# Conv and gated feed-forward on one core: the order of loads, casts and first convolutions in the opening

## The chip, the cores and the metric

The kernel runs on one NeuronCore of a Trainium2 chip. The metric is the device time in microseconds of one execution; the time before is 726.78 us, the median of five runs (726.22 to 727.24). The engines are TensorE (PE; its weight loads are shown as PEld), VectorE (DVE), ScalarE (ACT), GpSimd (Pool) and SyncE (SP). SP and ACT also issue the DMA transfers here, each from its own queue of instructions (SPq and ACTq in the profile).

## What is computed

A causal convolution of seven taps with softmax weights for each head, and then a feed-forward layer whose activation is h cos h:

```python
w = exp(weight - max) / sum                      # 8 heads x 7 taps, softmax over the taps
x_pad = concat(zeros(B, 6, D), x)                # B 8, S 4096, D 192, head h has 24 channels
a[b, s, h] = sum_k w[h, k] * x_pad[b, s + k, h]
h = a @ w_in                                     # 32768 x 192  @  192 x 2048
g = h * cos(h)
out = g @ w_out                                  # 2048 x 192
```

## The kernel before, in words

The 32768 tokens are 64 tiles of T = 512, two to a unit of 1024, so 32 units (NU). A unit is loaded as x_f (128 partitions, eight blocks of 128 tokens, and a ninth "edge" block with the 16 tokens around each block's start, which supplies the taps that reach back over the block's edge), cast to bf16 as x_bf (`cast_unit`, L182), and convolved on PE against `band`, a matrix with the tap weights on its diagonals (`conv_mm`, L195). The result goes from PSUM to `ct` by ACT (`conv_out`), Pool doubles it (`double_unit`, since the row halves of the array each want a copy), and a DMA transpose issued by SP turns it into `cT` (`turn_unit`), with channels on the partitions. Pool then mends the first six tokens of each block from the edge block.

For each tile there are eight pairs of feature blocks, j = 0 to 7. `mm1` (named h0 to h7 in the order strings) computes a pair into one of three double banks of PSUM, the ring `h_pool`; `gcu` (s0 to s7) takes its cosine on ACT into `cs` and multiplies on DVE into `g`, after which the ring's buffer is free. `mm2_step` (m with a count) multiplies g by w_out into two banks, o_p and o_q, a step at a time, one row half of the array for each of two phases that overlap. `evac` (P and Q) copies a finished bank to SBUF by ACT, and SP stores it.

The order is written by hand: PE_ORDER and ACT_ORDER from the third tile on, PE_FIRST and ACT_FIRST (L398, L400) for the first two. In these strings c1, c2 are the two parts of the convolution of channel half 1 and d1, d2 of channel half 0; ec and ed are their copies out of PSUM by ACT; r is `conv_rest`; p and q mark the ends of phases. A string's item is issued when those before it have been issued, and every engine works through its own instructions in that order. In the first tile (t = 0) the convolutions of unit 1 use the two o banks, so c waits for d's copies, and the first m steps wait for c's.

Where two matmuls on different row halves would add to the same bank, `Turn` (L166) orders them through SP: a no-operation on SP waits for the first matmul, and the second waits for it. That no-operation stands in SP's queue among its DMA issues, in program order.

The opening, which the change touches, is written out before the loop. Transfers: SP issues the first half of unit 0 (four blocks, 384 KB), half 0 of w_in's first half, the rest of unit 0, unit 1 (768 KB), its edges, the second half of w_in in two transfers (each fills 64 partitions, `load_w` L84), w_out in four. ACT issues the conv weights and half 1 of w_in's first half. PE runs matmuls on zeros (`keep_warm`, L112) and one small matmul that spreads the conv weights. Pool builds a mask and an identity; DVE, with one Exp on ACT (L154), computes the softmax, then `prod` and `diag` (L269, L272), and 16 small copies by the three engines place the diagonals into `band` (L277). ACT casts the first half of unit 0, Pool the second. DVE and Pool cast the first half of w_in (L281). Then `conv_first` convolves four blocks (L293) with copies by ACT and DVE (L299), `turn_first` transposes them on PE (L307), and the first tile starts. Pool's order from there: cast of unit 1 (L326), double of unit 0's second half, the second half of w_in (L435, all 1536 columns in one), w_out in two halves (L437).

Of the kernel before, what the change touches and what calls it, by code (L numbers as in the profile page):

```python
# [9 lines left out]
BF16 = mybir.dt.bfloat16  # L10
AF = mybir.ActivationFunctionType
# [5 lines left out]
def kernel(  # L17
# [8 lines left out]
    nc = tc.nc  # L26
    B, S, D = x.shape
    H, K = weight.shape
# [36 lines left out]
    x_tiles = {}  # L65


    def load_edges(u):
        nc.sync.dma_start(out=x_tiles[u][:, UB, :],  # L69
                          in_=xf[u * U - 8 : u * U - 8 + U, :].rearrange("(n t) d -> n t d", t=128)[:, 0:16, :])  # L70

    def load_unit(u, n0=0, n1=UB):
        if n0 == 0:
            x_tiles[u] = xin.tile([128, UB + 1, D], FP32, name="x_f")
        nc.sync.dma_start(out=x_tiles[u][:, n0:n1, :],  # L75
                          in_=xf[u * U + n0 * 128 : u * U + n1 * 128, :].rearrange("(n p) d -> p n d", p=128))


# [1 line left out]
    w_src = moe_w_in.rearrange("(m k) (t f) -> t m k f", k=NC, t=2)  # L80
    HP = NP // 2


    def load_w(q, queues):  # L84
        for t in range(2):
            queues[t].dma_start(out=w_f[64 * t : 64 * t + 64, :, q * HP : (q + 1) * HP, :].rearrange("p k j f -> p k (j f)"),
                              in_=w_src[t, :, :, q * HP * 128 : (q + 1) * HP * 128])

    load_unit(0, 0, NB)
    load_w(0, [nc.sync, nc.scalar])  # L90
    load_unit(0, NB, UB)
    load_unit(1)
    load_edges(1)
    load_w(1, [nc.sync, nc.sync])
    wo_f = consts.tile([128, NP, 2, D], FP32)
    wo_src = moe_w_out.rearrange("(i j p) d -> p j i d", i=2, p=128)

# [14 lines left out]
    def keep_warm(n):  # L112
        for _ in range(n):
            nc.tensor.matmul(out=idle, lhsT=zero[:, 0:128], rhs=zero, start=True, stop=True)  # L114
# [7 lines left out]
                            channel_multiplier=32)  # L122
    scrap = consts.tile([128, 1], FP32)
    nc.scalar.activation(out=scrap, in_=one, func=AF.Exp)  # L124
    keep_warm(3)
    w_all = o_pools[1].tile([128, T], FP32, name="o_ps1")
    w_bc = w_all[:, 0 : HQ * K].rearrange("p (h k) -> p h k", k=K)
    nc.tensor.matmul(out=w_all[:, 0 : HQ * K], lhsT=quarter, rhs=w_row, start=True, stop=True)
    keep_warm(17)


    xb0 = xbf_pool.tile([128, UB + 1, D], BF16, name="x_bf")

    E = 32 + K - 1
    mask = consts.tile([128, E, K], BF16)
    nc.gpsimd.memset(mask[0:32], 0.0)
    nc.gpsimd.affine_select(out=mask[0:32], in_=mask[0:32], compare_op=ALU.not_equal, fill=1.0, base=1 - K,
                            pattern=[[1, E], [1, K]], channel_multiplier=-1)
    for q in range(1, 4):
        nc.gpsimd.tensor_copy(out=mask[32 * q : 32 * q + 32], in_=mask[0:32])  # L140
    nc.gpsimd.memset(xb0[:, 0, :], 0.0)
    ident = consts.tile([128, 128], BF16)
    nc.gpsimd.memset(ident, 0.0)
    nc.gpsimd.affine_select(out=ident, in_=ident, compare_op=ALU.not_equal, fill=1.0, base=0, pattern=[[1, 128]],
                            channel_multiplier=-1)
    wn = consts.tile([128, HQ, K], BF16)
    band = consts.tile([128, H, 256], BF16)
    nc.vector.memset(band, 0.0)

    wmax = consts.tile([128, HQ, 1], FP32)  # L150
    nc.vector.tensor_reduce(out=wmax[:, :, 0], in_=w_bc, axis=mybir.AxisListType.X, op=ALU.max)
    wexp = consts.tile([128, HQ, K], FP32)
    nc.vector.tensor_tensor(out=wexp, in0=w_bc, in1=wmax.to_broadcast([128, HQ, K]), op=ALU.subtract)
    nc.scalar.activation(out=wexp, in_=wexp, func=AF.Exp)  # L154
    wsum = consts.tile([128, HQ, 1], FP32)
    nc.vector.tensor_reduce(out=wsum[:, :, 0], in_=wexp, axis=mybir.AxisListType.X, op=ALU.add)
    winv = consts.tile([128, HQ, 1], FP32)
# [21 lines left out]

    bf = {}  # L180

    def cast_unit(u, n0=0, n1=UB + 1):  # L182
        copy = nc.scalar.copy if u == 0 and n0 == 0 else nc.gpsimd.tensor_copy
        bf[u] = xb0 if u == 0 else xbf_pool.tile([128, UB + 1, D], BF16, name="x_bf")

        o = 1 if u == 0 else 0
        copy(out=bf[u][:, n0 + o : n1 + o, :].rearrange("p n (h k r) -> p (n h) k r", k=NC, r=R),  # L187
             in_=x_tiles[u][:, n0:n1, :].rearrange("p n (h r k) -> p (n h) k r", k=NC, r=R))
        if u and u % UPS == 0:
            nc.gpsimd.memset(bf[u][0:8, UB, :], 0.0)  # L190
        bf.pop(u - 2, None)
# [27 lines left out]
    def o_banks():  # L219
        return [o_pools[b].tile([128, T], FP32, name="o_ps%d" % b) for b in range(2)]  # L220

    def conv_part(u, c, banks):


        ps = banks()
        sides = [slice(0, 64), slice(64, 128)]

        def mm(i, rows, **flags):
            return conv_mm(u, c, ps, i, sides[rows], 0, UB + 1, **{"start": False, "stop": False, **flags})

        mm(0, 0, start=True)
        mm(2, 1, start=True)
        turn = Turn()
        turn.mark(mm(1, 0), mm(3, 1))
        yield
        turn.wait(mm(2, 0), mm(0, 1))
        mm(3, 0, stop=True)
        mm(1, 1, stop=True)
        yield
        if c == 0 and u not in ct_tiles:  # L240
            ct_tiles[u] = ct_pool.tile([128, UB + 1, NC, 2, 64], BF16, name="ct")
        for b in range(2):
            conv_out(u, c, ps, 0, 0, UB + 1, nc.scalar.copy, banks=(b,))
            yield
# [7 lines left out]
    def turn_unit(u, n0=0, n1=UB + 1):  # L252
        ct = ct_tiles.pop(u)
        if u not in cT:
            cT[u] = cT_pool.tile([128, UB + 1, NC, 128], BF16, name="cT")
        nc.sync.dma_start_transpose(out=cT[u][:, n0:n1].rearrange("p n c k -> p (n c) k"),
                                    in_=ct[:, n0:n1].rearrange("p n c t k -> p (n c t k)"))
        cT.pop(u - 2, None)

    def mend_edges(u):  # L260
# [2 lines left out]
                              in_=cT[u][:, UB].rearrange("p c (n t) -> p n c t", t=16)[:, :, :, 8 : 8 + K - 1])  # L263


    cast_unit(0, 0, NB)

    prod = consts.tile([128, HQ, E, K], BF16)
    nc.vector.tensor_tensor(out=prod, in0=mask.rearrange("p (o e) k -> p o e k", o=1).to_broadcast([128, HQ, E, K]),  # L269
                            in1=wn.rearrange("p h (o k) -> p h o k", o=1).to_broadcast([128, HQ, E, K]), op=ALU.mult)  # L270
    diag = consts.tile([128, HQ, E], FP32)
    nc.vector.tensor_reduce(out=diag, in_=prod, axis=mybir.AxisListType.X, op=ALU.add)  # L272
# [2 lines left out]
    for i in range(16):  # L275
        q, rows = divmod(i, 4)
        three[i % 3](out=band[32 * rows : 32 * rows + 32, HQ * q : HQ * (q + 1), 32 * rows : 32 * rows + E],  # L277
                     in_=diag[32 * q : 32 * q + 32])
    nc.scalar.activation(out=scrap, in_=one, func=AF.Sin)
    for k in range(NC):  # L280
        three[2 if k else 0](out=w[:, k, 0:HP], in_=w_f[:, k, 0:HP])  # L281
    cast_unit(0, NB, UB)
    ct_tiles[0] = ct_pool.tile([128, UB + 1, NC, 2, 64], BF16, name="ct")
    cT[0] = cT_pool.tile([128, UB + 1, NC, 128], BF16, name="cT")
# [38 lines left out]
    conv_first()  # L323
    turn_first(0)
    turn_first(1)
    cast_unit(1)  # L326
    load_unit(2)
    load_edges(2)


    g_tiles = {}
# [54 lines left out]
    def store(t, b0=0, b1=2):  # L386
# [8 lines left out]
    PE_ORDER = "h0 m7 c1 m6 c2 m4 h1 m7 q h2 h3 m12 h4 m10 h5 m10 h6 h7 p m8"  # L395
    ACT_ORDER = "s0 ec1 ec2 s1 Q s2 s3 s4 s5 P s6 s7"

    PE_FIRST = ["h0a h0b h1 r d1 h2 d2 h3 h4 h5 h6 c1 h7 c2 p m12",  # L398
                "h0 m8 h1 m12 q h2 h3 h4 m4 d1 m8 d2 h5 m8 h6 c1 m8 c2 h7 m4 p m8"]
    ACT_FIRST = ["s0a s0b s1 s2 ed1 ed2 s3 s4 s5 s6 ec1 ec2 s7", "s0 s1 s2 s3 s4 ed1 ed2 s5 s6 ec1 ec2 P s7"]  # L400

    HALVES = {"": (0, NB), "a": (0, NB // 2), "b": (NB // 2, NB)}
    step = 0
    for t in range(NT + 2):
        u, second = divmod(t, TPU)
        cu, cc = (u + TPU, second) if t >= TPU else (1 + t, 1)
        conv = {"c": conv_part(cu, cc, ring_banks if t else o_banks) if cu < NU else iter(())}
        if t < TPU:
            conv["d"] = conv_part(cu, 0, ring_banks if t else o_banks)
        act, done, h = (ACT_ORDER if t > 1 else ACT_FIRST[t]).split(), set(), {}  # L410

        def flush():
# [14 lines left out]

        for k in (PE_ORDER if t > 1 else PE_FIRST[t]).split():
            if k[0] == "h" and t < NT:
                h[k[1:]] = mm1(t, int(k[1]), *HALVES[k[2:]])  # L430
            elif k[0] in conv:
                next(conv[k[0]], None)
                if (t, k) == (0, "d1"):
                    turn_unit(0, NB, UB)
                    nc.gpsimd.tensor_copy(out=w[:, :, HP:NP], in_=w_f[:, :, HP:NP])  # L435
                    for q in range(2):
                        nc.gpsimd.tensor_copy(out=wo[:, q * HP : (q + 1) * HP], in_=wo_f[:, q * HP : (q + 1) * HP])  # L437
            elif k == "r":
                conv_rest()
                double_unit(0, NB, UB)  # L440
            elif k[0] == "m":
                for q in range(step, step + int(k[1:])):
                    mm2_step(q)
                step += int(k[1:])
            elif k[0] == "p":
                assert step % (2 * STEPS) == 0
            elif k[0] == "q":
                assert step % (2 * STEPS) == STEPS
            done.add(k)
# [61 lines left out]
```

## Time and profile before

| | us |
|---|---|
| median of five runs | 726.78 |
| the profiled execution's own time | 726.69 |
| span of its profile, first to last instruction | 725.0 |
| PE busy, share of the span | 711.7, 98% |
| DVE busy | 611.3, 84% |
| ACT busy | 618.0, 85% |
| Pool busy | 152.0, 21% |
| granted TensorE clock, mean | 0.995 |

How to read it: every line of a timeline has its start and its length in us from the first instruction, then engine, line, operation and the tiles written and read, and in square brackets how long the engine stood idle before and what it waited for. A chain line has start, length and what the time was spent on. A line of busy time by stage has the stage, its length, the busy us (and count) of PE, PEld, DVE, ACT and Pool, the granted share of the TensorE clock, the share of the 16 DMA engines that were busy, and GB/s. Ends of matmuls are modelled, so neighbouring PE lines overlap a little.

### The profile page before, as it was taken

Reading aid. Unit: us, or ns where it says so; the run is one execution under the profiler, and the core shown is the slowest. Engines: PE = TensorE matmul, PEld = TensorE weight load, DVE = VectorE, ACT = ScalarE, POOL = GpSimd, SP = SyncE. Lnnn points to the kernel's source line nnn. Section 1 sums busy time; section 2 is a strip of 40 time slices with the busy share of each in tenths; the row PEclk is TensorE's granted clock in tenths of the full one; section 3 lists DMA queues with packets and bytes.
Section 4 is the critical chain, followed back from the end, with each engine's and each line's share of the span. In section 5 each row is a group of like instructions: output and inputs, shape, how many; then the busy total and the mean of one; then the engine's idle time right before and its main releaser. Section 6 shows DMA issues by size and latency. Waiting matters only on the chain.

```text
span 725.0 us, 26371 instructions
## 1 busy us (share of the span) xinstructions
PE 711.7 (98%) x11848; PEld 531.4 (73%) x11848; DVE 611.3 (84%) x535; ACT 618.0 (85%) x781; POOL 152.0 (21%) x127
## 2 busy tenths in 40 slices
PE   7899999999999999999999999999999999999997
PEld 3477777777777777777777777777777777777776
DVE  5778888888888888888888888888888888888984
ACT  5788888888888888988988888888888888888883
POOL 6611222211222210222211222210222211221000
PEclk9899999999999999999999999999999999999999
DMA  9954344665344555444655343555443555323412
GB/s 212 221 125 121 102 110 100 143 143 123 104 113 93 144 143 121 103 120 89 143 143 124 110 116 88 139 144 127 109 118 87 136 143 133 107 71 87 80 47 66
DMA packets 184081, 86.04 MB, mean 119 GB/s; under 512 B 111648, under 2 KB 183200, under 8 KB 183968
## 3 DMA queue, kind: packets, MB, share of 16 engines
q1 hardware_dynamic: 183752, 83.96, 48.3%
q8 instruction: 92, 1.51, 0.8%
q10 hardware_dynamic: 216, 0.39, 0.2%
q14 instruction: 21, 0.17, 0.1%
HBM read 31.36 MB, written 25.17 MB: 78 GB/s over the span
## 4 chain that ended last, share of the span: by engine, by line
PE 95%; DMA 2%; DVE 1%; ACT 1%; SPq 1%; POOL 0%; issue 0%; DVEq 0%; POOLq 0%
PE o_ps L372 46%; PE h L342 45%; PE h L198 3%; DMA x_f<-in_x_dram 2%; DVE g L353 1%; ACT cs L349 1%; PE h L372 0%; POOL x_bf L187 0%; SPq L69 0%; SPq L75 0%; DVEq L506 0%; ACT o_sb L384 0%; POOL ct L250 0%; ACT ct L213 0%; PE o_ps L198 0%
## 5 line engine op out<-in xcount | busy, mean ns | idle before, releaser
L353 DVE TENSOR_TENSOR g<-h,cs 128x1024 bf16<-128x1024 f32 (+1 forms) x513 | 603.5, 1217 | 98.5 <-ACT cs L349 93.7
L349 ACT ACTIVATE cs<-h 128x1024 bf16<-128x1024 f32 (+1 forms) x513 | 511.8, 1026 | 62.4 <-PE h L342 55.2
L372 PE MATMUL o_ps<-wo,g 64*128 64x192 bf16 x8128 | 423.8, 243 | 1.8 <-ACT ct L213 0.6
L372 PEld LDWEIGHTS <-g 64*128 64x128 bf16 x8192 | 362.2, 94 | 85.5 <-SPq L171 1.2
L342 PE MATMUL h<-cT,w 64*128 64x512 bf16 (+1 forms) x3078 | 400.9, 377 | 0.7 <-DVE g L353 0.5
L342 PEld LDWEIGHTS <-w 64*128 64x128 bf16 x3078 | 155.3, 94 | 87.6 <-issue 3.9
L262 POOL COPY cT<-cT 128x144 bf16<-128x144 bf16 x31 | 9.6, 310 | 496.4 <-DMA cT<-ct 376.6
L187 POOL CAST x_bf<-x_f 128x1728 bf16<-128x1728 f32 (+1 forms) x32 | 80.5, 2518 | 2.4 <-DMA x_f<-in_x_dram 2.3
L213 ACT CAST ct<-h 128x432 bf16<-128x432 f32 x120 | 56.4, 522 | 28.1 <-PE h L198 26.8
L384 ACT COPY o_sb<-o_ps 128x384 f32<-128x384 f32 x127 | 60.0, 473 | 5.0 <-PE o_ps L372 5.0
L250 POOL COPY ct<-ct 128x1728 bf16<-128x1728 bf16 (+1 forms) x32 | 51.2, 1602 | 23.4 <-ACT ct L213 22.3
L198 PE MATMUL h<-x_bf,band 64*128 64x216 bf16 x480 | 43.0, 254 | 0.8 <-DVE g L353 0.5
L198 PEld LDWEIGHTS <-band 64*128 64x128 bf16 (+1 forms) x512 | 22.2, 94 | 9.4 <-issue 3.2
L114 PE MATMUL o_ps<-zero 128*128 128x512 bf16 x20 | 7.2, 531 | 1.3 <-DVE zero L109 1.3
L198 PE MATMUL o_ps<-x_bf,band 128*128 128x96 bf16 (+1 forms) x32 | 2.5, 245 | 4.1 <-POOL x_bf L187 2.7
L114 PEld LDWEIGHTS <-zero 128*128 128x128 bf16 x20 | 2.3, 126 | 4.8 <-issue 2.8
L372 PE MATMUL h<-wo,g 64*128 64x192 bf16 x64 | 5.8, 243 | 0.0
L213 ACT CAST ct<-o_ps 128x432 bf16<-128x432 f32 (+1 forms) x6 | 2.4, 456 | 1.1 <-PE o_ps L198 1.1
L437 POOL CAST wo<-wo_f 128x1536 bf16<-128x1536 f32 x2 | 2.9, 1469 | 1.9 <-DMA wo_f<-in_moe_w_out_dram 1.9
L124 ACT ACT_TABLE_LOAD x1 | 1.3, 1283 | 2.1 <-issue 2.1
L384 ACT COPY o_sb<-h 128x384 f32<-128x384 f32 x1 | 0.5, 479 | 2.4 <-PE h L372 2.4
L187 ACT CAST x_bf<-x_f 128x768 bf16<-128x768 f32 x1 | 1.2, 1224 | 1.4 <-DMA x_f<-in_x_dram 1.4
(47 smaller groups left out, 28.1 us busy)
## 6 DMA issues: line engine op xcount, KB each, us to landing
out_dram<-o_sb SPq DMA_DIRECT2D x63, 384.0 KB
x_f<-in_x_dram SPq DMA_DIRECT2D x31, 768.0 KB
x_f<-in_x_dram SPq DMA_DIRECT2D x31, 96.0 KB
wo_f<-in_moe_w_out_dram SPq DMA_DIRECT2D x4, 384.0 KB
w_f<-in_moe_w_in_dram SPq DMA_DIRECT2D x3, 384.0 KB
x_f<-in_x_dram SPq DMA_DIRECT2D x2, 384.0 KB
cT<-ct SPq DMA_TRANSPOSE x32
w_f<-in_moe_w_in_dram ACTq DMA_DIRECT2D x1, 384.0 KB
```

What stands on the lines that cost most here:

```text
L114: nc.tensor.matmul(out=idle, lhsT=zero[:, 0:128], rhs=zero, start=True, stop=True)
L187: copy(out=bf[u][:, n0 + o : n1 + o, :].rearrange("p n (h k r) -> p (n h) k r", k=NC, r=R), in_=x_tiles[u][:, n0:n1, :].rearrange("p n (h ...
L198: return nc.tensor.matmul(out=ps[i // 2][:, 0 : (n1 - n0) * 2 * G].rearrange("p (n k i r) -> p i n k r", n=n1 - n0, k=NC, i=2)[:, i % 2], ...
L213: copy(o[:, :, 0, :], i[:, :, 0, :])
L250: nc.gpsimd.tensor_copy(out=ct[:, n0:n1, :, 1, :], in_=ct[:, n0:n1, :, 0, :])
L262: nc.gpsimd.tensor_copy(out=cT[u][:, 0:UB, :, 0 : K - 1], in_=cT[u][:, UB].rearrange("p c (n t) -> p n c t", t=16)[:, :, :, 8 : 8 + K - 1])
L342: nc.tensor.matmul(out=h[:, i, n0 * 128 : n1 * 128], lhsT=w[rows, k, j, :], rhs=c[rows, m0 + n0 : m0 + n1, k, :], start=(k == 0), stop=(k ...
L349: nc.scalar.activation(out=cs[:, :, part], in_=h[:, :, part], func=AF.Sin, bias=math.pi / 2.0, scale=1.0)
L353: nc.vector.tensor_tensor(out=g_tiles[t][:, 2 * j : 2 * j + 2, part], in0=h[:, :, part], in1=cs[:, :, part], op=ALU.mult)
L372: m = nc.tensor.matmul(out=o_ps[tt, b][:, si * D : (si + 1) * D], lhsT=g_tiles[tt][rows, f, s * 128 : (s + 1) * 128], rhs=wo[rows, f // 2, ...
L384: nc.scalar.copy(o_sb[t][:, 2 * b : 2 * b + 2, :].rearrange("p s d -> p (s d)"), o_ps.pop((t, b))[:, 0 : 2 * D])
L437: nc.gpsimd.tensor_copy(out=wo[:, q * HP : (q + 1) * HP], in_=wo_f[:, q * HP : (q + 1) * HP])
```

## The change

- w_in comes in three pieces, columns of j 0 to 1, 2 to 3 and 4 to 7, each by two transfers of 64 partitions, all on SP; w_out follows them.
- Unit 1 and its edges are issued by ACT, after the warm-up Exp and before the softmax's Exp.
- 11 keep-warm matmuls follow the small matmul instead of 17.
- The mask has taps outside and positions inside; its three copies to the other partitions are on DVE, behind the clearing of band.
- The Sin table is loaded right after the softmax's Exp.
- The first half of unit 0 is cast in two parts, by ACT and by Pool; the first piece of w_in is cast by DVE, the second by Pool after the first transposes, the third in two parts by Pool after r.
- Unit 1's cast, the load of unit 2 and the transpose of unit 0's second half move to r, in the order shown.
- The convolutions of the first two tiles (units 1 and 2) run on all 128 rows with no turn. In the first tile d follows h5.

```diff
-    load_w(0, [nc.sync, nc.scalar])
+    load_w(0, 2)
     load_unit(0, NB, UB)
-    load_unit(1)
-    load_edges(1)
-    load_w(1, [nc.sync, nc.sync])
+    load_w(2, 4)
+    load_w(4, 8)
...
     nc.scalar.activation(out=scrap, in_=one, func=AF.Exp)
+
+    load_unit(1, queue=nc.scalar)
+    load_edges(1, queue=nc.scalar)
     keep_warm(3)
...
-    keep_warm(17)
+    keep_warm(11)
...
+    band = consts.tile([128, H, 256], BF16)
+    nc.vector.memset(band, 0.0)
     for q in range(1, 4):
-        nc.gpsimd.tensor_copy(out=mask[32 * q : 32 * q + 32], in_=mask[0:32])
+        nc.vector.tensor_copy(out=mask[32 * q : 32 * q + 32], in_=mask[0:32])
...
     nc.scalar.activation(out=wexp, in_=wexp, func=AF.Exp)
+    nc.scalar.activation(out=scrap, in_=one, func=AF.Sin)
...
-        mm(0, 0, start=True)
-        mm(2, 1, start=True)
-        turn = Turn()
-        turn.mark(mm(1, 0), mm(3, 1))
-        yield
-        turn.wait(mm(2, 0), mm(0, 1))
-        mm(3, 0, stop=True)
-        mm(1, 1, stop=True)
+        if whole:
+            for i in range(4):
+                conv_mm(u, c, ps, i, slice(0, 128), 0, UB + 1, start=i % 2 == 0, stop=i % 2 == 1)
+            yield
+        else:
...
-    cast_unit(0, 0, NB)
+    cast_unit(0, 0, NB // 2, nc.scalar.copy)
+    cast_unit(0, NB // 2, NB)
...
-    for k in range(NC):
-        three[2 if k else 0](out=w[:, k, 0:HP], in_=w_f[:, k, 0:HP])
+    nc.vector.tensor_copy(out=w[:, :, 0:2], in_=w_f[:, :, 0:2])
...
-    cast_unit(1)
-    load_unit(2)
-    load_edges(2)
+    nc.gpsimd.tensor_copy(out=w[:, :, 2:4], in_=w_f[:, :, 2:4])
...
-    PE_FIRST = ["h0a h0b h1 r d1 h2 d2 h3 h4 h5 h6 c1 h7 c2 p m12",
-                "h0 m8 h1 m12 q h2 h3 h4 m4 d1 m8 d2 h5 m8 h6 c1 m8 c2 h7 m4 p m8"]
-    ACT_FIRST = ["s0a s0b s1 s2 ed1 ed2 s3 s4 s5 s6 ec1 ec2 s7", "s0 s1 s2 s3 s4 ed1 ed2 s5 s6 ec1 ec2 P s7"]
+    PE_FIRST = ["h0a h0b h1 r h2 h3 h4 h5 d1 d2 h6 c1 c2 h7 p m12",
+                "h0 m8 h1 m12 q h2 h3 h4 m4 d1 d2 m8 h5 m8 h6 c1 c2 m8 h7 m4 p m8"]
+    ACT_FIRST = ["s0a s0b s1 s2 s3 s4 s5 ed1 ed2 s6 ec1 ec2 s7", "s0 s1 s2 s3 s4 ed1 ed2 s5 s6 ec1 ec2 P s7"]
...
-                if (t, k) == (0, "d1"):
-                    turn_unit(0, NB, UB)
-                    nc.gpsimd.tensor_copy(out=w[:, :, HP:NP], in_=w_f[:, :, HP:NP])
-                    for q in range(2):
-                        nc.gpsimd.tensor_copy(out=wo[:, q * HP : (q + 1) * HP], in_=wo_f[:, q * HP : (q + 1) * HP])
             elif k == "r":
                 conv_rest()
                 double_unit(0, NB, UB)
+                turn_unit(0, NB, UB)
+                for j in (4, 6):
+                    nc.gpsimd.tensor_copy(out=w[:, :, j : j + 2], in_=w_f[:, :, j : j + 2])
+                cast_unit(1)
+                load_unit(2)
+                load_edges(2)
+                for q in range(2):
+                    nc.gpsimd.tensor_copy(out=wo[:, q * HP : (q + 1) * HP], in_=wo_f[:, q * HP : (q + 1) * HP])
```

More of the change, by code (lines that the diff above doesn't have):

```diff
@@ L65, with load_edges, load_unit @@
     x_tiles = {}
-    def load_edges(u):
-        nc.sync.dma_start(out=x_tiles[u][:, UB, :],
+    def load_edges(u, queue=nc.sync):
+        queue.dma_start(out=x_tiles[u][:, UB, :],
                           in_=xf[u * U - 8 : u * U - 8 + U, :].rearrange("(n t) d -> n t d", t=128)[:, 0:16, :])
-    def load_unit(u, n0=0, n1=UB):
+    def load_unit(u, n0=0, n1=UB, queue=nc.sync):
         if n0 == 0:
             x_tiles[u] = xin.tile([128, UB + 1, D], FP32, name="x_f")
-        nc.sync.dma_start(out=x_tiles[u][:, n0:n1, :],
+        queue.dma_start(out=x_tiles[u][:, n0:n1, :],
                           in_=xf[u * U + n0 * 128 : u * U + n1 * 128, :].rearrange("(n p) d -> p n d", p=128))
@@ L81, with load_w @@
     HP = NP // 2
-    def load_w(q, queues):
+    def load_w(j0, j1):
         for t in range(2):
-            queues[t].dma_start(out=w_f[64 * t : 64 * t + 64, :, q * HP : (q + 1) * HP, :].rearrange("p k j f -> p k (j f)"),
-                              in_=w_src[t, :, :, q * HP * 128 : (q + 1) * HP * 128])
+            nc.sync.dma_start(out=w_f[64 * t : 64 * t + 64, :, j0:j1, :].rearrange("p k j f -> p k (j f)"),
+                              in_=w_src[t, :, :, j0 * 128 : j1 * 128])
     load_unit(0, 0, NB)
-    load_w(0, [nc.sync, nc.scalar])
+    load_w(0, 2)
     load_unit(0, NB, UB)
-    load_unit(1)
-    load_edges(1)
-    load_w(1, [nc.sync, nc.sync])
+    load_w(2, 4)
+    load_w(4, 8)
     wo_f = consts.tile([128, NP, 2, D], FP32)
@@ L128 @@
     nc.tensor.matmul(out=w_all[:, 0 : HQ * K], lhsT=quarter, rhs=w_row, start=True, stop=True)
-    keep_warm(17)
+    keep_warm(11)
     xb0 = xbf_pool.tile([128, UB + 1, D], BF16, name="x_bf")
     E = 32 + K - 1
-    mask = consts.tile([128, E, K], BF16)
+    mask = consts.tile([128, K, E], BF16)
     nc.gpsimd.memset(mask[0:32], 0.0)
     nc.gpsimd.affine_select(out=mask[0:32], in_=mask[0:32], compare_op=ALU.not_equal, fill=1.0, base=1 - K,
-                            pattern=[[1, E], [1, K]], channel_multiplier=-1)
+                            pattern=[[1, K], [1, E]], channel_multiplier=-1)
+    band = consts.tile([128, H, 256], BF16)
+    nc.vector.memset(band, 0.0)
     for q in range(1, 4):
-        nc.gpsimd.tensor_copy(out=mask[32 * q : 32 * q + 32], in_=mask[0:32])
+        nc.vector.tensor_copy(out=mask[32 * q : 32 * q + 32], in_=mask[0:32])
     nc.gpsimd.memset(xb0[:, 0, :], 0.0)
@@ L146 @@
     wn = consts.tile([128, HQ, K], BF16)
-    band = consts.tile([128, H, 256], BF16)
-    nc.vector.memset(band, 0.0)
     wmax = consts.tile([128, HQ, 1], FP32)
@@ L180, with cast_unit @@
     bf = {}
-    def cast_unit(u, n0=0, n1=UB + 1):
-        copy = nc.scalar.copy if u == 0 and n0 == 0 else nc.gpsimd.tensor_copy
+    def cast_unit(u, n0=0, n1=UB + 1, copy=nc.gpsimd.tensor_copy):
         bf[u] = xb0 if u == 0 else xbf_pool.tile([128, UB + 1, D], BF16, name="x_bf")
@@ L220, in o_banks, with conv_part @@
         return [o_pools[b].tile([128, T], FP32, name="o_ps%d" % b) for b in range(2)]
-    def conv_part(u, c, banks):
+    def conv_part(u, c, banks, whole=False):
         ps = banks()
@@ L229, in mm @@
             return conv_mm(u, c, ps, i, sides[rows], 0, UB + 1, **{"start": False, "stop": False, **flags})
-        mm(0, 0, start=True)
-        mm(2, 1, start=True)
-        turn = Turn()
-        turn.mark(mm(1, 0), mm(3, 1))
-        yield
-        turn.wait(mm(2, 0), mm(0, 1))
-        mm(3, 0, stop=True)
-        mm(1, 1, stop=True)
+        if whole:
[3 more added lines that the diff above has]
+        else:
+            mm(0, 0, start=True)
+            mm(2, 1, start=True)
+            turn = Turn()
+            turn.mark(mm(1, 0), mm(3, 1))
+            yield
+            turn.wait(mm(2, 0), mm(0, 1))
+            mm(3, 0, stop=True)
+            mm(1, 1, stop=True)
         yield
@@ L263, in mend_edges @@
                               in_=cT[u][:, UB].rearrange("p c (n t) -> p n c t", t=16)[:, :, :, 8 : 8 + K - 1])
-    cast_unit(0, 0, NB)
+    cast_unit(0, 0, NB // 2, nc.scalar.copy)
+    cast_unit(0, NB // 2, NB)
     prod = consts.tile([128, HQ, E, K], BF16)
-    nc.vector.tensor_tensor(out=prod, in0=mask.rearrange("p (o e) k -> p o e k", o=1).to_broadcast([128, HQ, E, K]),
+    nc.vector.tensor_tensor(out=prod, in0=mask.rearrange("p k (o e) -> p o e k", o=1).to_broadcast([128, HQ, E, K]),
                             in1=wn.rearrange("p h (o k) -> p h o k", o=1).to_broadcast([128, HQ, E, K]), op=ALU.mult)
@@ L278 @@
                      in_=diag[32 * q : 32 * q + 32])
-    nc.scalar.activation(out=scrap, in_=one, func=AF.Sin)
-    for k in range(NC):
-        three[2 if k else 0](out=w[:, k, 0:HP], in_=w_f[:, k, 0:HP])
+    nc.vector.tensor_copy(out=w[:, :, 0:2], in_=w_f[:, :, 0:2])
     cast_unit(0, NB, UB)
@@ L406 @@
         cu, cc = (u + TPU, second) if t >= TPU else (1 + t, 1)
-        conv = {"c": conv_part(cu, cc, ring_banks if t else o_banks) if cu < NU else iter(())}
+        conv = {"c": conv_part(cu, cc, ring_banks if t else o_banks, t < TPU) if cu < NU else iter(())}
         if t < TPU:
-            conv["d"] = conv_part(cu, 0, ring_banks if t else o_banks)
+            conv["d"] = conv_part(cu, 0, ring_banks if t else o_banks, True)
         act, done, h = (ACT_ORDER if t > 1 else ACT_FIRST[t]).split(), set(), {}
```

## The prediction

> **What bounds the kernel now.** I read the page's slices first, then the chain of waits over the opening, then the timeline of each engine there. In slices of 18 us, TensorE (PE) is full from the third on:
>
> ```profile
> PE   7899999999999999999999999999999999999997
> PEclk9899999999999999999999999999999999999999
> ```
>
> From 41 us a tile of 512 tokens repeats every 10.85 us with PE busy throughout; nothing in the diff reaches that part. So the change can only move the moment at which the steady state begins. The chain shows what that moment hangs on:
>
> ```profile
> 2.68 11.64 DMA x_f<-in_x_dram
> 14.37 1.94 POOL x_bf L187
> ...
> 17.94 1.71 SPq L69
> ...
> 19.76 0.54 PE o_ps L198 x4
> ...
> 26.28 0.53 ACT ct L213
> 26.81 0.05 issue
> 26.85 0.99 PE o_ps L372 x10
> ```
>
> Unit 1 lands (14.3), Pool casts it, PE does d1; d2 waits for the turn on SP, which stands behind a transfer of unit 2; the o banks are emptied by ACT, and only then the first m steps start (26.85). On PE (start, length, idle before):
>
> ```profile
> 13.34 0.85 PE L198 MATMUL o_ps<-x_bf,band 128*128 128x96 bf16 x16
> 16.91 0.36 PE L198 MATMUL o_ps<-x_bf,band 64*128 64x216 bf16 x4 [2.72 <-POOL x_bf L187]
> 17.09 1.26 PE L342 MATMUL h<-cT,w 64*128 64x512 bf16 x6
> 19.76 0.54 PE L198 MATMUL o_ps<-x_bf,band 64*128 64x216 bf16 x4 [1.40 <-SPq L171]
> 20.09 4.77 PE L342 MATMUL h<-cT,w 64*128 64x512 bf16 x24
> ```
>
> The 24 matmuls of h3 to h6 took 1.2 us a group of six, against 0.65 later (1.29 for twelve in the chain). Busy time by stage says why: the granted clock (after the busy columns, 0.50) was halved for two stages after the idle one.
>
> ```profile
> 13.93:17.35 3.42, 0.70 (x15) 0.54 (x13) 1.98 (x4) 0.98 (x3) 2.98 (x2) 1.00 1.10 186
> 17.35:20.76 3.41, 2.01 (x14) 0.68 (x12) 1.23 (x1) 1.44 (x3) 1.76 (x3) 0.50 1.10 324
> 20.76:24.17 3.41, 3.41 (x18) 1.17 (x16) 1.44 (x2) 2.57 (x4) 2.63 (x2) 0.50 1.27 306
> ```
>
> Pool's casts show when the second half of w_in and each half of w_out land (each waited for its DMA):
>
> ```profile
> 18.19 1.47 POOL L435 CAST w<-w_f 128x1536 bf16<-128x1536 f32 x1 [0.56 <-DMA w_f<-in_moe_w_in_dram]
> 20.75 1.47 POOL L437 CAST wo<-wo_f 128x1536 bf16<-128x1536 f32 x1 [1.09 <-DMA wo_f<-in_moe_w_out_dram]
> ```
>
> The transfers never pause (share about 1 from 3 to 24 us), at two rates, last column GB/s: w_in alone at 4 to 5 us, x at 9 to 10.5.
>
> ```profile
> 4.00:5.00 1.00, 1.00 (x4) 0.39 (x3) 0.82 (x4) 0.00 (x0) 0.87 (x4) 1.00 0.97 205
> 9.00:10.50 1.50, 1.02 (x32) 0.91 (x31) 0.84 (x2) 1.22 (x3) 0.92 (x2) 1.00 1.10 328
> ```
>
> **What the Trainium skill says.** "TensorE: Matmul & The Clock Gate", Part 1: the clock halves after a largely idle window of 3.413 us and returns after a busy one, windows running freely. The trace agrees: halved for 6.83 us, two windows, after one with PE 20% busy; 59% busy did not restore it, 100% did. "SBUF — State Buffer", Door 1: a transfer into partitions 0 to 63 reaches half of the ports, some 218 GB/s. Agrees with 205. "DMA: Bandwidth & Descriptors", Issuing engines are not separate DMA queues: ACT's transfers share SP's 16 engines. Agrees: ACT's half of w_in did not raise the rate. "ScalarE: Activation LUTs", What ACT_TABLE_LOAD costs: about 1.28 us; the trace has 1.28.
>
> **The change, part by part.**
>
> *To the first conv.* Keep-warm matmuls held PE to 8.97, though ACT's last band copy ended at 7.92. Now 11 follow: PE free by 3.23 + 11 x 0.43 = 8.0. ACT: the table load moves up to 1.4 as its w_in issue goes; with the warm Exp, 2.9; then unit 1 and its edges are issued there, by SP's rows 0.55 + 0.73, to 4.2. Behind that stands the Exp of L154 (before 3.74), and DVE's sums and the band wait for it. From that Exp to the end of diag was 2.15 us; the strided mask read may add 0.15 (0.47 to 0.62 for 532 elements; below nothing is excluded, the work is the same): diag ends 6.5 instead of 5.89. Mask copies on DVE: 3 x 0.2 to 0.4 (its 32x76 casts took 0.26, Pool's copies 0.40), all before 4.2: nothing. The Sin table, 1.28 + 0.20, now precedes the cast: 4.4 to 5.9. ACT's half cast, 0.65 (half of 1.22), to 6.55, Pool's beside it; five band copies 1.35, to 8.0; DVE's six, 1.6, to 8.15. First conv 8.2 instead of 9.02: 0.8 earlier. If the edges' issue blocks ACT (SP's w_in issues took about 2 us each at 4 us[...]) it is 0.7 later. Both ends are covered, see below.
>
> *First convs to r.* 9.02 to 14.19 was 5.17; so r ends at 13.4. The new DVE cast of w (0,2), 0.43 x 1.5 = 0.65, lies between its band copies (8.15) and its ct copy (9.3). Pool's double ends about 16.3.
>
> *Transfers.* Up to the last piece of w_in the bytes are the same set (x0, w_in, unit 1, edges), so it lands at the same **18.1**; only the order ahead changes. Unit 1 no longer stands after x0 on SP but comes in by ACT near 3 us; w (2,4), half of the old second w_in cast's bytes, lands about 14.2 (18.1 less w (4,8)'s 786 KB at 205 GB/s, 3.9). Bounds on 18.1: mixing unit 1 with w_in could lift 205 towards 328 for at most 0.88 MB, up to 1.5 us earlier; the other end is rival D. SP's queue: unit 1 and edges (1.3 us of issues) leave it, two small w_in issues are added; w_out still follows all of w_in; unit 2 now goes behind the transpose (about 4.2 us of SP), which waits for Pool's double (16.3): issued about 21 instead of 14.4. Its data had to follow w_out (22.9) anyway, and its cast is Pool's after double_unit(1); it must be done by d1 of tile 1, about 32. I cost it at nothing; if it came 2 us later than 30, tile 1 would wait.
>
> *h2 to the o banks.* Pool: w (2,4) 0.82 (between 0.61 for 512 elements and 1.47 for 1536), to 15.05; h2, h3 by 16.4. Then w (4,6), w (6,8) at 18.15: to 19.0 and 19.8; only now unit 1, 2.5, to **22.35**. On PE h4, h5 at 19.0 to 20.3, then d at 22.35: five us later than before, but whole, with no turn. With the clock full: d 0.36, ACT's two copies 0.94 to 23.7; h6 23.4; s6 1.02 to 24.7; c after the copies; ec1 0.52, so m at **25.25**, 1.6 before 26.85. With the clock halved to 24.2: d 0.72, copies to 24.05, h6 1.28, s6 to 25.4, m at 25.95: 0.9 earlier. Halved to 27.6, PE is the limit: c, h7 to 26.4, and twelve m steps at 0.16 instead of 0.08 end 0.15 later than before. PE is busy only 30% from 13.4 to 22.35, so a halved clock is likely again; I take **0.7** out of -0.15 to 1.6. w_out's casts fall to 22.4 to 25.3 on Pool: the first 12 steps use the first half only (23.9), in time.
>
> *Tile 1.* Its four turns go, and d1, d2 stand together:
>
> ```profile
> 35.36 0.36 PE L198 MATMUL h<-x_bf,band 64*128 64x216 bf16 x4 [0.35 <-SPq L171]
> ...
> 38.98 0.82 PE L342 MATMUL h<-cT,w 64*128 64x512 bf16 x6 [0.28 <-DVE g L353]
> ```
>
> Now d2 came 1.4 us after d1 (33.99): m8, then the turn. ACT's copies waited till 35.8, s5 behind them till 36.6, g5 ended 38.94, and h7 needs its buffer. Changed, on the old clock: d 33.99 to 34.35, copies 34.5 to 35.45, m8, h5 to 35.65, s5 to 36.7, g5 to 37.9, h7 at 37.95: **1.0** earlier. Nothing else is late then: PE's own work from 33.99 to h7 sums to 3.96. Least gain 0.35, the one wait.
>
> Sum: 0.7 + 1.0 = 1.7 off 726.69, the profiled run (span 725.0 and 1.7 around it), which stands 0.1 under the median of 726.78: **725.0**.
>
> **Rivals.**
> - A, the forecast. For: each wait has its row. Against: the late d1 may keep the clock down. 725.0, from 724.1 (full clock) up. Chance 0.47.
> - B, the clock: two idle stretches of about 2 to 2.6 us (16.4 to 19.0, 20.3 to 22.35) hold it at half to 27.6. For: one stretch of 2.72 was enough before. The first gain is gone, the second stays at least in part: 0.85 or less, 725.9 to 726.5. Chance 0.26.
> - C, unit 1 and w_in flow together and w_in ends up to 1.5 us earlier; against, two halves on two queues did not add up before. 723.6. Chance 0.08.
> - D, slower: w_in's new pieces have rows of 1 KB instead of 2 KB for half its bytes. At 205 GB/s a 2 KB row takes an engine 160 ns; if that is a price per row, not per byte, 24 more rows per engine cost 24 x 160 = 3.84 us, w_in ends at 22 and d is at 26.2; m at 29.1, 2.25 late, less 1.0 in tile 1: 727.9. It decides from 134 ns a row (2.6 us). Against: x's 768 B rows take 38 ns at 328 GB/s. Unit 1 coming between w_in's pieces in some dearer way acts at the same place. Chance 0.19.
>
> **How the numbers follow.** A measurement of this kernel tells about 0.2% (1.45 us) from no change. Faster by more: most of A and C, 0.43 + 0.08 = 0.51. Within: the rest of A's chance and most of B, 0.29. Slower: D and a little of B, 0.20. The range 723.5 to 727.5 leaves out C's far end and most of D, under 0.2.
>
> **What would show it.** Right: Pool's cast of w (4,6) still starts at about 18.1, unit 1's at 19.8, d at 22.3, first m step at 25.2 to 26.4, no SP turn before tile 2, h7 of tile 1 about a us sooner after d1. Wrong: the w (4,6) cast past 20 (D) or before 17 (C); the clock at half beyond 25 (B); conv first later than 10, which would break the cover ahead of w (2,4).

## The result, and the profile after

The changed kernel takes 725.84 us (median of 26 runs) beside 726.70 for the kernel before (47 runs): a ratio of 0.9986, 95% interval 0.9981 to 0.9991. That is 1.0 us faster, 0.6 to 1.4: clear of no change, on the right side, and less than the 1.7 forecast. It is 0.14%, under the 0.2% that the prediction took as the least it could tell from no change, so what came true is its "within" (chance 0.29) and not its "faster by more" (0.51). The profiled execution took 725.81, its span 724.1 against 725.0.

The slices of the page after (PE busy and granted clock, in tenths):

```profile
PE   7799999999999999999999999999999999999997
PEclk9999999999999999999999999999999999999999
```

The second slice no longer has an 8 in its clock row, but its PE busy is lower. The chain of waits of the changed kernel over the opening (start, length, work):

```profile
2.06 8.73 DMA w_f<-in_moe_w_in_dram
...
10.88 0.69 DVE w L286
11.58 0.87 DVE ct L304
...
20.30 0.83 POOL w L442
21.13 2.07 POOL x_bf L188
23.19 0.33 issue
23.52 2.89 POOL wo L447 x2
26.41 0.03 issue
26.45 1.00 PE o_ps L376 x10
```

Before, the chain began with unit 1's transfer. Now it begins with the *first* piece of w_in, which holds DVE to 10.88, and runs through Pool. On PE:

```profile
12.49 0.34 PE L312 MATMUL h<-ident,ct 128*128 128x128 bf16 x3 [2.00 <-DVE ct L304]
...
15.69 1.23 PE L199 MATMUL o_ps<-x_bf,band 128*128 128x96 bf16 x16
...
20.41 1.47 PE L346 MATMUL h<-cT,w 64*128 64x512 bf16 x12 [2.09 <-POOL w L442]
23.63 0.53 PE L199 MATMUL o_ps<-x_bf,band 128*128 128x216 bf16 x4 [1.75 <-POOL x_bf L188]
```

r stands at 15.69 (before 13.34, forecast to end at 13.4), unit 1's convolution at 23.63 (forecast 22.35), the first m step at 26.45 (before 26.85). Three idle stretches of PE, of about 2 us each, where before there were two. In the second tile:

```profile
33.58 0.54 PE L199 MATMUL h<-x_bf,band 128*128 128x216 bf16 x4 [0.49 <-DVE g L357]
34.06 0.83 PE L376 MATMUL o_ps<-wo,g 64*128 64x192 bf16 x16
...
37.92 0.81 PE L346 MATMUL h<-cT,w 64*128 64x512 bf16 x6
```

h7 is at 37.92 instead of 38.98, 1.06 earlier: 0.40 of it was there at the first m step, and 0.66 comes from this tile. The whole 1.06 is still there where the third tile takes over (39.66 against 40.72), and 0.9 of it at the end of the spans.

Why the first tile is late stands in ACT's timeline, where ACTq rows are its DMA issues:

```profile
1.43 1.28 ACT L122 ACT_TABLE_LOAD   x1 [1.43 <-PEq L502]
1.50 0.42 ACTq L75 DMA_DIRECT2D x_f<-in_x_dram  x1
1.95 0.72 ACTq L69 DMA_DIRECT2D x_f<-in_x_dram  x1
```

In the kernel's text unit 1's load stands behind the warm Exp, which ran at 2.72, when the table load had ended. The trace has its issue at 1.50, while the table load ran. So its 864 KB came in among the first piece of w_in and the rest of unit 0.

### The profile page after: what moved, and what is told of

It reads as the page before. It is cut to its first block, busy times and chain, and to the rows that moved or that the text cites. A ratio compares the mean times of both kernels' runs of the same rounds, so it can differ in the third digit from the quotient of the medians.

```text
span 724.1 us, 26324 instructions
## 1 busy us (share of the span) xinstructions
PE 709.5 (98%) x11826; PEld 530.2 (73%) x11826; DVE 613.5 (85%) x538; ACT 617.3 (85%) x781; POOL 150.4 (21%) x125
## 3 DMA queue, kind: packets, MB, share of 16 engines
q8 instruction: 92, 1.51, 0.8%
## 4 chain that ended last, share of the span: by engine, by line
PE 96%; DMA 1%; POOL 1%; ACT 1%; DVE 1%; issue 0%; DVEq 0%; SPq 0%; POOLq 0%
PE o_ps L376 46%; PE h L346 45%; PE h L199 3%; DMA w_f<-in_moe_w_in_dram 1%; ACT cs L353 0%; PE h L376 0%; POOL wo L447 0%; DVE g L357 0%; POOL x_bf L188 0%; POOL w L442 0%; PE o_ps L199 0%; DVEq L513 0%; ACT o_sb L388 0%; DVE ct L304 0%; DVE w L286 0%
## 5 line engine op out<-in xcount | busy, mean ns | idle before, releaser
L188 POOL CAST x_bf<-x_f 128x1728 bf16<-128x1728 f32 (+2 forms) x33 | 81.2, 2461 | 5.0 <-DMA x_f<-in_x_dram 5.0
L199 PE MATMUL h<-x_bf,band 64*128 64x216 bf16 (+1 forms) x472 | 42.7, 254 | 0.5 <-DVE g L357 0.5
L112 PE MATMUL o_ps<-zero 128*128 128x512 bf16 x14 | 5.5, 561 | 1.3 <-DVE zero L107 1.3
```

Source lines behind the costliest of these rows:

```text
L199: return nc.tensor.matmul(out=ps[i // 2][:, 0 : (n1 - n0) * 2 * G].rearrange("p (n k i r) -> p i n k r", n=n1 - n0, k=NC, i=2)[:, i % 2], ...
```

## The experiments

The main theory, Q, was that unit 1 comes too early on ACT's queue and makes the first tile late. The rival, L, was that the first tile has slack and the end of w_in, Pool's casts and unit 1 decide. Later the granted clock, theory K, was tested by itself. Medians of the kernel before beside these runs were 726.64, 726.49 and 726.80 in the three sets.

**Unit 1 back on SP, ahead of the third piece of w_in.**

```diff
-    load_unit(1, queue=nc.scalar)
-    load_edges(1, queue=nc.scalar)
...
     load_w(2, 4)
+    load_unit(1)
+    load_edges(1)
     load_w(4, 8)
```

> Unit 1 and its edges go back from ACT's queue to SP's, behind the second piece of w_in and ahead of the third; all else as in the changed kernel. Theory Q (on ACT's queue unit 1 was issued at 1.50 us and its packets took engine time from the first piece of w_in and the rest of unit 0, which landed at 10.8 and 12.4, so the first tile ran late and Pool reached the third piece only at 19.5): the first piece lands near 8, the rest of unit 0 near 9, h0 starts near 11 instead of 12.96, Pool's cast of w (4,6) at about 18 instead of 19.52, unit 1's convolution near 22.2 instead of 23.63, and the time falls by about 1.4 us, to 724.4. Rival L (the start of the first tile has slack; what costs is the late end of w_in, then Pool's three casts, then unit 1): h0 is earlier but unit 1's convolution stays at 23.3 to 23.6, time 725.6 to 725.9.

Measured: 727.25 us, 1.4 *slower* than the changed kernel; ratio to before 1.0007 (0.9994 to 1.0021). (The times below are of an execution of 729.70, in runs from 725.22 to 730.88.) The first tile did what Q says: h0 at 10.79, r at 12.44. But Pool then waited for the third piece:

```profile
21.16 1.60 POOL L442 CAST w<-w_f 128x768 bf16<-128x768 f32 x2 [4.84 <-DMA w_f<-in_moe_w_in_dram]
```

PE stood idle for 7.36 us ahead of h4. An early first tile was worth nothing by itself here: Q's number fails, L's mechanism stands, and neither foresaw that the third piece would end at 21.

**Unit 1 on SP behind all of w_in.** The same edit, with the two lines behind `load_w(4, 8)`.

> Unit 1 and its edges on SP behind all of w_in and ahead of w_out. Theory Q: as in the run before for the first tile; the third piece of w_in now lands near 14.5 and unit 1 near 17.8, so Pool goes on from its double at about 17 without a pause, unit 1 is cast by 21.4 and convolved then; first m step near 24.3, 2.1 us sooner than the changed kernel: 723.7. Rival L, in which Pool's double at 18.75 to 19.6 stays where it is: at most 0.5 sooner, 725.3.

Measured: 723.85, ratio to before 0.9957 (0.9941 to 0.9973); 2.0 faster than the changed kernel. Pool's casts, and the first m step on PE:

```profile
16.27 1.60 POOL L442 CAST w<-w_f 128x768 bf16<-128x768 f32 x2
18.17 2.50 POOL L188 CAST x_bf<-x_f 128x1728 bf16<-128x1728 f32 x1 [0.30 <-DMA x_f<-in_x_dram]
20.63 1.46 POOL L447 CAST wo<-wo_f 128x1536 bf16<-128x1536 f32 x1
22.68 1.47 POOL L447 CAST wo<-wo_f 128x1536 bf16<-128x1536 f32 x1 [0.60 <-DMA wo_f<-in_moe_w_out_dram]
```

```profile
24.03 1.65 PE L376 MATMUL o_ps<-wo,g 64*128 64x192 bf16 x10
```

Bytes now arrive in the order in which Pool casts them, and its two waits in these lines are 0.30 and 0.60 us. The m step also settles a reading: the changed kernel's chain names Pool's w_out casts ahead of its m step (26.41), but here the step starts at 24.03 while the second of these casts runs to 24.15. What it waited for in the changed kernel was c's copy on ACT, the first part of which ran from 25.88 to the same 26.40; in the run with zeros below, the same m step is shown waiting for this copy.

**DVE's cast of the first piece behind the first transposes.** Transfers as in the changed kernel.

```diff
-    nc.vector.tensor_copy(out=w[:, :, 0:2], in_=w_f[:, :, 0:2])
     cast_unit(0, NB, UB)
...
     turn_first(1)
+    nc.vector.tensor_copy(out=w[:, :, 0:2], in_=w_f[:, :, 0:2])
```

> DVE's cast of the first piece of w_in moves behind the copies of the first transposes; the transfers are as in the changed kernel. Theory Q with the head of DVE's queue as its means (that cast waited to 10.88 for its transfer, and the copy of the first convolution stood behind it): the copy is at about 9.4 instead of 11.58, h0 starts at about 11.7 instead of 12.96, r ends near 14.8 instead of 16.8, Pool's cast of w (4,6) starts at 17.9 instead of 19.52; time about 1.3 less, 724.5. Rival L: h0 is earlier, the time stays within 0.3 of 725.8.

Measured: 725.17, 0.7 less than the changed kernel, half of what Q says; ratio to before 0.9976 (0.9968 to 0.9984). h0 started at 12.5 and r at 14.9, but Pool waited 1.3 us for the third piece (cast at 19.13). So by the times of h0 and r the waiting cast at the head of DVE's queue is a part of the lateness, and the end of w_in bounds what its removal brings. Where the 0.7 us lie is not shown: the profiled execution is the slowest of the 22 (726.88), its clock was halved from about 20.6 to 27.2, and its first m step came at 27.53, later than the changed kernel's 26.45.

**Whole-row convolutions alone, in the kernel before.** `conv_part` as in the change for tiles 0 and 1; loads, casts and order strings as before.

> The kernel before, with one part of the change alone: convolutions of units 1 and 2 on all 128 rows with no turn, the order strings as before. If the turns are what the change gained: d2's wait of 1.40 in the first tile and 0.35 in the second go, the m steps after the second tile start about 1.0 us sooner, time 725.6 to 725.9. If a matmul on all rows costs as much more as the turns did (0.12 us each instead of 0.09): 726.5 to 726.9.

Measured: 724.45, ratio 0.9965 (0.9950 to 0.9980): 2.2 us from this part alone (seven runs, 724.00 to 725.36), more than the 725.6 to 725.9 expected and more than the whole change. Its first m step is at 25.87, 0.98 sooner than before; its third tile takes over at 39.20, 1.52 sooner; its span is 1.8 shorter.

**Unit 1 on SP ahead of the third piece, with the clock held up.** The first kernel of these, and:

```diff
+            elif k[0] == "w":
+                keep_warm(int(k[1:]), h_pool.tile([128, 2, T], FP32, name="h")[:, 0, :])
...
-    PE_FIRST = ["h0a h0b h1 r h2 h3 h4 h5 d1 d2 h6 c1 c2 h7 p m12",
+    PE_FIRST = ["h0a h0b h1 r h2 h3 w18 h4 h5 w8 d1 d2 h6 c1 c2 h7 p m12",
```

> The kernel with unit 1 on SP between the second and the third piece of w_in (727.25 us, with TensorE idle for 7.4 us ahead of h4 and the clock halved for four windows after it), and matmuls on zeros put into its two idle stretches: 18 ahead of h4 and 8 ahead of unit 1's convolution, into a buffer of the ring that nobody reads. Theory K (that kernel lost to the changed one by the clock, which its long pause halves just when the second tile needs it): the clock stays full from 8 us on, time 725.0 to 725.8, no more than the changed kernel's. Rival W (it lost because on one queue the third piece of w_in lands later, 20 to 21 us instead of 17.8): the clock is full and the time falls by less than 0.7, to 726.6 or more, with Pool's cast of w (4,6) still at 20 or later.

Measured: 726.05, between the two; ratio to before 1.0002 (0.9991 to 1.0012). The profile's clock is full from 7 us on, and Pool's cast still starts at 21.10. By the medians 1.2 of the 1.4 lost to the changed kernel came back with the clock, but the ratios with and without the zeros overlap, and runs with a mean clock of 0.999 or more still spread from 724.1 to 728.6. So the share of the clock is not settled here, and something besides the clock varies. What is shown is that with a full clock this kernel is still not faster than the changed one: its third piece is still late, with PE idle for 3.06 us even so.

**Unit 1 behind w_in, with the clock held up.** The same with w9 and w8.

> The kernel with unit 1 behind all of w_in (723.85 us), and matmuls on zeros in its two idle stretches: 9 ahead of h4 and 8 ahead of unit 1's convolution. Theory K: the window that was at half clock from 21.98 to 25.39 is full, the copies of c end at the same time but h7 and the first m steps are no longer slow, and the spread of the runs shrinks: 722.6 to 723.2. Rival (the zeros hold up h4 or the convolution by as much as they save, since each takes 0.22 us and a buffer of the ring): 723.7 to 724.3.

Measured: 722.49, ratio 0.9948 (0.9935 to 0.9961), five runs from 722.48 to 722.95. The first m step is at 23.25:

```profile
23.25 0.99 PE L376 MATMUL o_ps<-wo,g 64*128 64x192 bf16 x10 [0.30 <-ACT ct L214]
```

It took 0.99 for ten, against 1.65 in the kernel without the zeros, where the clock was halved from 22.0 to 25.4. This is the best version: 3.4 us under the changed kernel. The ratios with and without the zeros overlap, but all five runs lie under five of the other six (722.44 to 724.62), and the traces agree with the difference of 1.4 in the medians: the third tile takes over at 36.46 instead of 37.90.

**The turns put back into the changed kernel.** `conv_part` without its whole-row form for tiles 0 and 1.

> The changed kernel with the turns put back: the convolutions of units 1 and 2 on two row halves again, d1 and d2 and c1 and c2 side by side as in its order strings. If the turns are where the change gained (alone they gave 2.2 us): each of the four turns costs a round by SP of about 0.35 us, and half-row matmuls save 0.11 us a part: about 1.0 more, 726.8; with SP's transfers standing ahead of a turn in the first tile up to 1.4 more, 728.2. If the gain comes from the new order of loads and casts instead: 725.6 to 726.1.

Measured: 728.04, ratio to before 1.0030 (1.0019 to 1.0042). Two of its turns on PE, in an execution of 731.79 whose clock was halved from 24.3 to 37, so that the second is not typical:

```profile
23.27 0.36 PE L199 MATMUL o_ps<-x_bf,band 64*128 64x216 bf16 x4 [0.80 <-SPq L173]
...
39.95 0.36 PE L199 MATMUL h<-x_bf,band 64*128 64x216 bf16 x4 [1.09 <-SPq L173]
```

With whole rows alone and the kernels before and changed this makes a square:

| | turns | whole rows | difference |
|---|---|---|---|
| loads, casts and order as before | 726.5 to 726.8 | 724.45 | -2.2 |
| loads, casts and order as changed | 728.04 | 725.84 | -2.2 |
| difference | +1.4 | +1.4 | |

By the medians whole rows gain 2.2 in either row, and all the rest of the change together *costs* 1.4, what the clock took included. The signs are clear, the sizes less so. By the ratios whole rows alone gain 2.5 us (1.5 to 3.6), and the rest alone costs 2.2 (1.4 to 3.1) while the two together gain 1.0; so it is not shown that the parts add up exactly, and an interaction of about a us is not excluded.

**Whole rows in the second tile alone, in the kernel before.**

> The kernel before, with whole-row convolutions in the second tile alone (unit 2); unit 1's keep their turns. The run with both gave 724.45. If the second tile's turn is worth what the changed kernel's trace shows there (0.66 us from the first m step to the end of the tile): 725.9 to 726.1, and unit 1's turns, which stood behind SP's transfers for 1.4 us, are worth the other 1.5. If it is all in the second tile: 724.5 to 725.0.

Measured: 725.71, ratio 0.9991 (0.9985 to 0.9998). So the second tile's turns are worth 0.65 us by the ratio (0.15 to 1.1) and 0.8 by the medians. The traces agree: from the first m step to the third tile's takeover it is 13.87 us before, 13.22 here and 13.21 in the changed kernel. Unit 1's turns are then the other 1.3 to 1.5 of the 2.2, as a difference between sets of runs, good to about a us.

**The changed kernel with the clock held up.** The edit as above, with w9 and w6, and 7 zeros between `turn_first(0)` and `turn_first(1)`.

> The changed kernel with matmuls on zeros in its three idle stretches and nothing else: 7 between the two halves of the first transposes, 9 ahead of h4, 6 ahead of unit 1's convolution, each lot into a buffer of the ring that nobody reads. Theory K (part of the missing gain is the clock: among the changed kernel's own runs those with a mean clock of 0.998 or 0.999 took 723.9 to 724.5, those with 0.993 took 726.5): 724.2 to 724.6, with fewer runs far from the median. Rival (the clock halves where TensorE waits for others anyway): 725.6 to 726.0.

Measured: 724.72, ratio 0.9973 (0.9965 to 0.9982), runs from 724.26 to 725.51. The first tile is still late and the first m step at 26.20. So about 1 us of the changed kernel's time is the clock: 1.1 by the medians, 0.9 (0.2 to 1.6) by the ratios. The changed kernel's own executions say the same: nine with a mean clock of 0.993 took 726.5 on average, sixteen with 0.995 to 0.997 725.6, two with 0.998 and 0.999 took 723.9 and 724.5.

**Unit 1's edges alone behind the third piece.** The first kernel of these, with `load_edges(1)` behind `load_w(4, 8)`.

> The kernel with unit 1 on SP between the second and the third piece of w_in (727.25 us; its third piece landed at 21.0 in two profiles, against 17.8 with unit 1 on ACT's queue), with unit 1's edges alone moved behind the third piece. If the edges' transfer, which uses half of the DMA engines, holds the third piece up: it lands near 18.5 and the time is 725.0 to 725.6. If it is unit 1 itself, or the single queue: landing at 20 or later, 727.0.

Measured: 725.83, 1.4 under the first kernel; ratio to before 0.9984 (0.9976 to 0.9992).

```profile
18.43 1.60 POOL L442 CAST w<-w_f 128x768 bf16<-128x768 f32 x2 [2.09 <-DMA w_f<-in_moe_w_in_dram]
```

In the profiles the third piece lands 2.7 us earlier for a move of 96 KB: Pool's cast starts at 18.43, against 21.16 and 21.10 in the two runs with the edges in front. The traces have eight completions for a load of edges and sixteen for every other load, and in the first kernel those of the last piece came spread from 16.76 to 21.04, against 16.31 to 17.82 in the changed one. That fits edges that stand in front on half of the DMA engines; the runs show the delay, and this reason for it is argued.

**Unit 1 on ACT's queue, issued behind the softmax's Exp.**

```diff
-    load_unit(1, queue=nc.scalar)
-    load_edges(1, queue=nc.scalar)
...
     nc.scalar.activation(out=wexp, in_=wexp, func=AF.Exp)
+    load_unit(1, queue=nc.scalar)
+    load_edges(1, queue=nc.scalar)
```

> The changed kernel with unit 1 and its edges still on ACT's queue, but issued behind the softmax's Exp (3.8 us) instead of ahead of it, where they were issued at 1.50. That is nearer to the order that the forecast assumed (issue at 2.9 to 4.2, behind the first piece of w_in and unit 0). Theory Q (the early issue is what made the first tile late): the first piece of w_in lands near 8 instead of 10.8, h0 starts near 11 instead of 12.96, the third piece still ends near 18, time 724.7 to 725.3, about the forecast. Rival L (the first tile's lateness is covered, the end of the third piece decides): 725.6 to 726.1, or more if the third piece lands later than 18.

Measured: 725.60, ratio to before 0.9990 (0.9982 to 0.9997), not apart from the changed kernel: L's number, not Q's. The first piece was there by 8.37, Pool's cast of w (4,6) at 18.20 and unit 1's convolution at 22.30, almost exactly the forecast's times. ACT stood behind its own DMA issue,

```profile
5.42 0.71 ACTq L69 DMA_DIRECT2D x_f<-in_x_dram  x1
6.17 1.28 ACT L156 ACT_TABLE_LOAD   x1 [2.00 <-DMA w_f<-in_moe_w_in_dram]
```

so that its band copies ended at 9.63 instead of 8.44, and the second piece of w_in was waited for (cast at 13.23 after 2.17), but the cast was still 1.0 earlier than in the changed kernel. What took the gain back stands on PE:

```profile
22.30 0.53 PE L199 MATMUL o_ps<-x_bf,band 128*128 128x216 bf16 x4 [1.75 <-POOL x_bf L188]
...
25.30 1.80 PE L376 MATMUL o_ps<-wo,g 64*128 64x192 bf16 x10
```

The first m step came 1.15 earlier than the changed kernel's 26.45, inside the forecast's 25.25 to 25.95. But the clock was halved from 23.9 to 27.3, the ten m steps took 1.80 instead of 1.00, and the third tile took over at 39.48 instead of 39.66: 0.18 of the 1.15 is left. No run held the clock up in this kernel, so that rests on this one trace.

## Why the prediction came out as it did

*The sum.* Forecast 0.7 + 1.0 = 1.7; measured 1.0 (0.6 to 1.4). Both terms were too large, and what lies under the first was a gain and a loss that I had not kept apart: by the medians, unit 1's turns +1.3 to 1.5, the new order -1.4. 725.84 lies between A's 725.0 and the 725.9 to 726.5 of B, next to B. That it came so near was in part luck: unit 1's convolution came 1.28 late, and the clock, which I had priced as likely halved, was full at that moment, so the first m step stood at 26.45 against 26.15 (26.85 - 0.7) in spite of a wrong walk up to it.

*The step that failed first* is the issue by ACT: "with the warm Exp, 2.9; then unit 1 and its edges are issued there". They were issued at 1.50, beside the table load. The softmax's Exp was therefore on time (3.80, not 4.2), and the first piece of w_in was not: I had DVE's cast of it "between its band copies (8.15) and its ct copy (9.3)", hidden; it waited to 10.88, and the ct copy behind it to 11.5. So r came 2.4 later than before instead of 0.8 earlier, Pool's double ended at 19.6 instead of 16.3, and the cast of w (4,6), which I had bound to the landing at 18.15, was bound to Pool at 19.52. The later issue restores these times and brings the first m step 1.15 earlier, so the lateness did cost what stands ahead of that step. The medians differ by only 0.24, which is within their spread; in the trace the halved clock over the m steps took the rest.

*The end of w_in* was right: forecast 18.1; the completions in the trace put it at 17.8. Rival D, a price per row, is out: half of w_in came in 1 KB rows and it ended no later. Two of my workings around it were wrong: with 24 more rows an engine, 2.6 us are 108 ns a row and not 134, and at 4 to 5 us w_in was not alone, since ACT's cast of x at 5.32 still waited for its transfer. Behind unit 1's landing, from 15 to 17 us, the rate was 151 to 187 GB/s. That unit 1's place could move it by 3 us (17.8, 18.4, 21.0) I had only as D's last sentence. C, for mixing, had it at 0.3, not 1.5.

*Unit 1's convolution* came 1.28 later than forecast (23.63), the m step 2.82 after it (forecast 2.9 with the clock full). From there the walk was right. Of the signs I had named, the absence of SP turns came true. Pool's cast of w (4,6) at 19.52 (for 18.1), unit 1's at 21.07 (for 19.8), the convolution, and the m step at 26.45 (for 25.2 to 26.4) were all late, and none was late enough for a sign of being wrong.

*The clock* (rival B) was right in kind and wrong in place. In the profiled execution it was halved from 13.1 to 16.5, behind the idle stretch at 10.5 that I had not foreseen, and full at 24:

```profile
13.93:17.35 3.42, 3.42 (x34) 1.87 (x32) 1.88 (x3) 2.39 (x5) 0.83 (x1) 0.62 1.08 212
```

Over the runs it cost about 1 us, near the 0.9 between my full-clock case and the 0.7 that I took. "TensorE: Matmul & The Clock Gate", Part 1, has the windows running freely; the spread of one kernel's runs along their clock (726.5 at 0.993, about 724.2 at 0.998 and above) agrees with that.

*Tile 1*: 0.66 in the trace and 0.65 to 0.8 alone, instead of 1.0. The mechanism was as described; the mis-sized term is the whole-row convolution: 33.58 to 34.06 is 0.48 for four matmuls, where I had 0.36 from the half rows, twice in this tile. That is 0.24 of the missing 0.34; PE ran without a gap from 33.58 to 37.92, 4.34 us where I had 3.96, and the remaining 0.1 is open.

*What I costed at nothing*: unit 2, loaded later (issued at 22.0, forecast 21), held nobody up; w_out's casts, though named in the chain, did not either; mask copies on DVE, 0.84 in all, ended at 3.36 and held the softmax's first step back by 0.06. Prod was not nothing: 1.17, where I had bounded the strided read at 0.62, and the row ahead of it took 0.66 instead of 0.17; diag ended at 7.06 instead of 6.5.

## What to carry to other kernels

Order transfers by the order in which one consumer works them off, and price a load that is moved ahead by what stands behind it, also on other queues; here the same bytes in two orders on two queues were 2.0 us apart, and on one queue 3.4. Split a compound change into a square of runs before explaining it: a gain of 1.0 was about 2.2 from one part and a loss of about 1.4 from the rest. An idle stretch of TensorE can cost its length and then a halved clock (of the three in the changed kernel's profile the first was followed by one): where work can't be moved in, matmuls on zeros into a free buffer gave back 1.1 to 1.4 us by the medians.

## What the runs showed of the hardware that was not expected

- A DMA issue that follows an ACT_TABLE_LOAD in ACT's program did not wait for it: issued at 1.50 in a load that ran from 1.43 to 2.71. The other way round a table load stood behind an issue: it started at 6.17, the issue ahead of it ran from 5.42 to 6.13 (unit 1 issued later on ACT).
- DVE's multiply of 532 bf16 elements took 0.47 us with both inputs read densely and 1.17 with one read at a stride of 38 elements, with Pool idle throughout (from 5.08 to 7.20):

```profile
4.45 0.66 DVE L161 TENSOR_TENSOR wn<-wexp,winv 128x14 bf16<-128x14 f32 x1
5.15 1.17 DVE L276 TENSOR_TENSOR prod<-mask,wn 128x532 bf16<-128x532 bf16 x1
```

- The row above it took 0.17 before. It ran while Pool cast x (4.39 to 5.08) and ended with it; where Pool's cast started during prod instead, the cast took 1.51 instead of 0.69 and prod the same 1.17 (unit 1 on SP). "SBUF — State Buffer", Who interferes with whom, says that a DVE instruction with two SBUF inputs contends with a GpSimd instruction that reads SBUF; both rows agree, each way round.
- A load of 96 KB with eight completions, ahead of a transfer with sixteen, put that transfer's end off by 2.7 us (21.16 against 18.43 for the cast that waits for it, one profile each).
